# C and B loaded in pairs of chunks, first loads reordered, V loaded once, first products on VectorE

## Chip, cores and metric

The kernel runs on one core of a Trainium2 chip. The metric is the device time of one execution in microseconds. The times before are the median of three runs.

## What is computed

A Mamba-like mixer of 4 batches, 8 heads, 768 tokens, head width 32 and state width 16 works in chunks of 32 tokens; two feed-forward stages of width 1024 follow, the second after a mixing of the tokens through U and V of rank 32.

```python
# mixer, chunk by chunk: la = log(a)
L = np.exp(cum[:, :, :, None] - cum[:, :, None, :]) * causal
CB = np.einsum('bhin,bhjn->bhij', Cc, Bc)
y_intra = np.einsum('bhij,bhjd->bhid', CB * L, xc)
y_inter = np.einsum('bhin,bhnd->bhid', Cc, state) * decay_to_i[:, :, :, None]
state = decay_full[:, :, None, None] * state + np.sum(Bx, axis=2)
# first feed-forward stage
xn = (x - mu) / np.sqrt(var + 1e-06) * g_ln
x = x + np.maximum(xn @ w_ch1, 0.0) @ w_ch2
# second stage
h = x.transpose(0, 2, 1) @ U @ V
u = x + h.transpose(0, 2, 1)
out = u + np.maximum(u @ w_ch1, 0.0) @ w_ch2
```

The weights, U and V come as 64-bit floats, and the kernel turns them into 32-bit ones; the two stages' weights and V are then split into a high and a low part.

## The kernel before, in words

Everything is one list of work items. `Plan.add` (L81) takes a name, an engine, a planned cost, a function that issues the instructions, and the items it waits for. `Plan.issue` (L90) runs a small model of the engines, picks the item that is due first among those that could start soon, and calls its function: the order that it finds is the order of the instructions on every engine, and each engine works through its own in that order. A load is planned with a cost on SP's queue and one on a shared wire (`sp`, L49); constants such as `LAT`, `PER` and `SHIFT` (L41, L54) belong to this model alone. `FIRST` (L28) gives the first loads due times ahead of all others, in that order; those in `ACTQ` (L31) are issued from ScalarE's queue. `POOL` (L33) lists the items that GpSimd does instead of VectorE. Up to a planned time of 28 us the plan puts fillers (`dummy`, L997) on TensorE wherever its next item is planned more than 0.5 us ahead (L155 to L159); their number is fixed when the program is built.

The 768 tokens of a batch are 6 chunks of 128, so there are 24 chunks. In the first two batches (`FINE`) a chunk is worked in two halves of 64 tokens. For a chunk `bc` brings the decays into `lt` or, for the first two chunks, from `r` through a product into `bcp` (L557), after a clip and a memset on `r` (L405, L568); `scan` (L601) runs along them; `cb` (L610) multiplies C and B from `stk`; `mult` (L622) makes `mm` from both; `bw` (L634) and `stm` (L708) are the products for the state; `state` (L679, into `sps`) and `intra` (L657, L664, into `yps`) are the products on TensorE; `tps`, `mean`, `var` turn the result and take its moments.

`stk` before is two tiles, for even and odd chunks. Three loads fill one for a chunk (L577 to L584): B for 32 rows, and C for the even and the odd heads beside zeros that `stkz` has written once. The load of chunk k waits for `cb` of chunk k-2. For batches 2 and 3 the same tiles are cleared again (`stk0`) and filled from stacks in memory.

A weight piece is converted by `to_f32` (L295): the load into one of three `raw` slots, `a` on ScalarE, `s` (a shift, L315), `o` and `f` (L319) on VectorE. `w1_piece` of the first layer goes through TensorE (`pc`, L341 and L354) with `gd` and `gm`; the others are split on ScalarE and VectorE. V (L384 to L397) is loaded four times into the four groups of 32 rows, for each half. `ra` and `rcb` (L428 to L438) are the decays and C in rows of head and state; a clip (L405) and a scan (L447) on VectorE and a copy into `starts` on GpSimd (L442) belong to them.

The feed-forward stages run as `mm1` (L818, `hps`), `hh` and `hl` (L825, L829) and `mm2` (L843, L849, `acc`), interleaved over the batches by `ORDER` (L37).

## Time and profile before

| | us |
|---|---|
| median of three runs | 387.43 (387.12 to 388.31) |
| the profiled execution | 387.38 |
| its span | 385.5 |
| TensorE busy | 371.6 |
| VectorE busy | 249.7 |
| ScalarE busy | 154.2 |
| GpSimd busy | 10.1 |

The span runs from the first to the last instruction. PE is TensorE's matmuls, PEld its weight loads, DVE VectorE, ACT ScalarE, POOL GpSimd, SP the engine whose queue issues most loads. L and a number name a line of the kernel. PEclk is the granted clock of TensorE as a share of 2.4 GHz. A float32 product shows as two matmul instructions.

### The profile page before, as it was taken

What the parts mean: (1) busy time and instruction counts of PE and PEld (TensorE: products, weight loads), DVE (VectorE), ACT (ScalarE), POOL (GpSimd) and SP (SyncE); (2) the same over time, 40 slices, a digit from 0 to 9 for tenths busy, and PEclk for the clock granted to TensorE, in tenths of its full rate; (3) what the DMA queues carried; (4) which work ended last, traced back from release to release, by engine and by line L of the source; (5) the groups of instructions that cost most, each with busy time, mean ns of one, the idle gap of its engine ahead of it and who ended that gap; (6) DMA issues with size and microseconds to landing.
All of it is one profiled execution on the core that took longest, in us unless ns stands there. A gap on an engine that the chain in (4) does not pass through costs nothing.

```text
span 385.5 us, 8399 instructions
## 1 busy us (share of the span) xinstructions
PE 371.6 (96%) x3389; PEld 318.8 (83%) x3389; DVE 249.7 (65%) x512; ACT 154.2 (40%) x402; POOL 10.1 (3%) x28
## 2 busy tenths in 40 slices
PE   5999899989999999999999999999999999999996
PEld 2787788778888879998987779999878789998895
DVE  5798879989973894683563889258942742434232
ACT  3173653464634632433422541235432561233231
POOL 2202000000000100000000000000000000000000
PEclk9999999969999999999999999999999999999999
DMA  5776770656020683680032442219120010000010
GB/s 153 247 229 205 211 211 21 184 148 199 26 98 11 247 320 116 199 308 3 18 106 81 135 133 86 94 33 266 41 61 0 32 45 2 0 2 28 2 54 30
DMA packets 32243, 42.23 MB, mean 110 GB/s; under 512 B 4248, under 2 KB 21448, under 8 KB 32204
## 3 DMA queue, kind: packets, MB, share of 16 engines
q1 hardware_dynamic: 31772, 41.33, 34.6%
q8 instruction: 27, 0.44, 0.4%
q10 hardware_dynamic: 432, 0.37, 0.3%
q14 instruction: 12, 0.10, 0.1%
HBM read 33.72 MB, written 7.95 MB: 108 GB/s over the span
## 4 chain that ended last, share of the span: by engine, by line
PE 76%; DVE 12%; DMA 8%; issue 2%; ACT 1%; SPq 0%; ACTq 0%; DVEq 0%
PE hps L818 30%; PE acc L849 16%; PE acc L843 15%; DVE lt L601 3%; DMA lt<-arows 3%; DMA raw<-in_w 2%; PE yps L664 2%; DVE hl L829 2%; DMA rcb<-in_cbT 2%; PE cb L610 2%; DVE w L319 2%; PE cb L615 1%; PE ups L929 1%; DVE mm L622 1%; DMA ra<-in_a_rep 1%
## 5 line engine op out<-in xcount | busy, mean ns | idle before, releaser
L829 DVE SCALAR_TENSOR_TENSOR hl<-hps,hh 128x256 fp32r<-128x256 f32 (+1 forms) x128 | 70.4, 552 | 94.2 <-ACT hh L825 94.1
L825 ACT ACTIVATE hh<-hps 128x256 fp32r<-128x256 f32 (+1 forms) x128 | 62.6, 490 | 142.1 <-PE hps L818 127.1
L818 PE MATMUL hps<-yhl,w 128*128 128x512 f32 (+1 forms) x384 | 78.5, 341 | 0.3 <-DVE yhl L233 0.3
L818 PE MATMUL hps<-uhl,w 128*128 128x256 f32 (+1 forms) x384 | 77.1, 339 | 0.0
L843 PE MATMUL acc<-w,hh 128*128 128x256 f32 x384 | 73.6, 287 | 0.3 <-DVE w L233 0.3
L849 PE MATMUL acc<-hh,w 128*128 128x512 f32 (+1 forms) x256 | 73.5, 339 | 0.0
L818 PEld LDWEIGHTS hps<-uhl,w 128*128 128x128 f32 x384 | 61.0, 190 | 8.9 <-issue 1.0
L843 PEld LDWEIGHTS acc<-w,hh 128*128 128x128 f32 x384 | 62.2, 193 | 4.8 <-ACT hh L825 1.3
L818 PEld LDWEIGHTS hps<-yhl,w 128*128 128x128 f32 x384 | 59.5, 190 | 7.1 <-DVE yhl L233 0.7
L843 PE MATMUL acc<-w,hl 128*128 128x256 f32 x192 | 55.0, 286 | 1.0 <-DVE hl L829 1.0
L849 PEld LDWEIGHTS acc<-hh,w 128*128 128x128 f32 x256 | 46.2, 190 | 5.6 <-ACT hh L825 0.4
L601 DVE TENSOR_TENSOR_SCAN lt<-lt,eye 128x512 f32<-128x512 f32 x34 | 41.1, 1216 | 5.0 <-DMA lt<-arows 4.9
L849 PE MATMUL acc<-hl,w 128*128 128x512 f32 (+1 forms) x128 | 43.2, 337 | 0.1
L843 PEld LDWEIGHTS acc<-w,hl 128*128 128x128 f32 x192 | 37.0, 193 | 1.5 <-DVE hl L829 1.4
L849 PEld LDWEIGHTS acc<-hl,w 128*128 128x128 f32 x128 | 24.3, 190 | 2.5 <-DVE hl L829 0.3
L622 DVE TENSOR_TENSOR mm<-cb,lt 128x512 f32<-128x512 f32 x36 | 23.7, 684 | 1.6 <-PE cb L615 0.8
L319 DVE SCALAR_TENSOR_TENSOR w<-raw,w 128x512 int32<-128x512 int32 (+2 forms) x38 | 24.5, 650 | 0.1
L230 ACT ACTIVATE w<-raw 128x512 f32<-128x512 f32 (+2 forms) x19 | 12.2, 643 | 13.1 <-DMA raw<-in_w 8.6
L664 PE MATMUL yps<-mm,xt 128*32 128x64 f32 (+1 forms) x576 | 16.3, 246 | 1.2 <-issue 1.2
L610 PE MATMUL cb<-stk 32*64 32x128 f32 x192 | 14.4, 298 | 0.6 <-DMA stk<-in_cbT 0.6
L664 PEld LDWEIGHTS yps<-mm,xt 128*32 128x32 f32 x576 | 10.9, 112 | 4.0 <-issue 1.5
L610 PEld LDWEIGHTS cb<-stk 32*64 32x64 f32 x192 | 11.8, 147 | 2.6 <-issue 1.1
(101 smaller groups left out, 354.2 us busy)
## 6 DMA issues: line engine op xcount, KB each, us to landing
raw<-in_w SPq DMA_DIRECT2D x16, 512.0 KB, 4.6
lt<-arows SPq DMA_DIRECT2D x12, 512.0 KB, 4.7
stk<-st SPq DMA_DIRECT2D x48, 96.0 KB, 2.4
st<-sh SPq DMA_DIRECT2D x8, 384.0 KB, 8.1
xt<-in_xb SPq DMA_DIRECT2D x14, 192.0 KB, 3.3
lt<-arows SPq DMA_DIRECT2D x20, 128.0 KB, 4.3
out<-u SPq DMA_DIRECT2D x8, 256.0 KB, 2.1
xt<-in_xb SPq DMA_DIRECT2D x20, 96.0 KB, 3.2
```

The source lines that it names most:

```text
L230: A.activation(out=out, in_=in_, func=AF.Copy, **kw)
L319: V.scalar_tensor_tensor(out=t, in0=words(w), scalar=scalar, in1=t, op0=op, op1=ALU.bitwise_or)
L601: V.tensor_tensor_scan(t, pair[k] if k < 2 else t, eye, 0.0, op0=ALU.mult, op1=ALU.add)
L610: P.matmul(p[r_, 2 * q * w_:2 * (q + 1) * w_], t[:32, q, 0, r_], t[:32, q, 1:3, r_], start=True, stop=True, skip_group_check=True)
L615: P.matmul(p[:, 2 * q * C:2 * (q + 1) * C], stk[k % 2][:, pr, 0, :], stk[k % 2][:, pr, 1:3, :], start=True, stop=True)
L622: V.tensor_tensor(out=mm_[k][:, s_], in0=cbp[k, hf], in1=lt[k][:, s_], op=ALU.mult)
L664: P.matmul(p[32 * q:32 * q + 32, e, cols], x_[:, xh:xh + D], mm_[k][:, h * w_:(h + 1) * w_], start=q not in begun, stop=True, skip_group_c ...
L818: P.matmul(p[:, :n], w[:, k, fs], x[:, k, :], start=(i == 0), stop=(i == 5))
L825: A.activation(out=hh[:, :n], in_=hps[l, key, f][:, :n], func=AF.Relu)
L829: V.scalar_tensor_tensor(out=hl[:, :n], in0=hps[l, key, f][:, :n], scalar=0.0, in1=f32(hh[:, :n]), op0=ALU.max, op1=ALU.subtract)
L843: P.matmul(p, x[:, t * C:(t + 1) * C], w[:, f, :], start=(f == 0 and i == 0 and t % 2 == 0), stop=(f == NF - 1 and i == 2), skip_group_che ...
L849: P.matmul(accs[l, key][d][:, :n], w[:, f, ds_], x[:, :n], start=(f == 0 and i == 0), stop=(f == NF - 1 and i == 2))
```

## The change

- `stk` becomes one tile of four strips of 32 rows, each with the two chunks of a pair side by side. Three loads fill a strip for two chunks, and the odd chunk has no load of its own. `stkz` clears the tile's zeros, one half on VectorE and one on GpSimd. The load of a pair waits for `cb` of the chunks seven and eight back. `cb` reads its strip.
- `FIRST` is reordered and has two more loads; the first piece of `w1` is issued from ScalarE's queue, after `ra` and `rcb`.
- V is loaded once into 32 rows, converted there, and ScalarE writes its high part twice.
- `bw` and `stm` of chunks 0 and 1 move from GpSimd to VectorE; `starts` and a `stk` memset move to GpSimd, two memsets of `xt` to VectorE.
- The model's constants change, and it counts the loads in flight; the first items may be waited for longer.

Empty lines are left out of the diff.

```diff
--- before.py
+++ after.py
@@ -25,12 +25,12 @@
 FINE = sum(n == 2 for n in NS)
 PARTS = ((0, 2), (2, NC))
-FIRST = [('bc0', 0), 'cst0', ('stk', 0), ('ra', 0, 0), ('stk', 1), (('w1', 0, 0), 'ld'), ('xb', 0), ('rcb', 0, 0), 'cst',
-         'rows', (('w2', 0, 0), 'ld'), (('w1', 0, 1), 'ld')]
-ACTQ = ['cst0', ('ra', 0, 0), ('rcb', 0, 0)]
-POOL = {'rac': (), 'bw': (0, 1, 3, 4), 'stm': (0, 1, 4, 2)}
+FIRST = [('bc0', 0), 'cst0', ('ra', 0, 0), ('rcb', 0, 0), ('stk', 0), ('xb', 0), (('w1', 0, 0), 'ld'), 'cst', 'rows',
+         (('w2', 0, 0), 'ld'), (('w1', 0, 1), 'ld'), ('ra', 0, 2), ('stk', 2)]
+ACTQ = ['cst0', ('ra', 0, 0), ('rcb', 0, 0), (('w1', 0, 0), 'ld')]
+POOL = {'rac': (), 'bw': (3, 4), 'stm': (4, 2)}
 PE_SPLIT = ()
 YT = (2, 2)
@@ -38,7 +38,7 @@
          "000 001 010 101 011 020 100 111 021 110 030 121 031 120 131 130".split()]
-LAT, PER, T0, NEAR, SWITCH, STAY = 0.2308, 1.1979, 14.0, 0.2, 0.11, 3.0
+LAT, PER, T0, NEAR, SWITCH, STAY = 0.294, 1.1979, 14.0, 0.2, 0.047, 3.18
 dve = lambda n: 0.065 + n / 960
 scn = lambda n: 0.06 + n / 480
 dve2 = lambda n: 0.065 + n / 1920
@@ -46,12 +46,14 @@
 act = lambda n: 0.093 + n / 1200
 actp = lambda n: 0.051 + n / 1200
 pool_tt = lambda n: 0.0024 * n
-sp = lambda n, kb: (0.5 * n, kb / 360)
+sp = lambda n, kb: (0.5 * n, kb / RATE)
+RATE, FLIGHT = 290, 8
 SP_FIRST, SP_LAST = 0.65, 0.92
-SHIFT = dict(zip("rows w0 w1 w2 ra0 ra chunk0 chunk".split(), [-0.01, -2.48, 0.87, 6.97, -1.94, -0.4, -0.61, -1.17]))
+FIRST_NEAR = 2.0
+SHIFT = dict(zip("rows w0 w1 w2 ra0 ra chunk0 chunk".split(), [1.23, -2.48, 1.08, 6.97, -1.61, -2.81, -0.61, -1.17]))
 def kind(n):
@@ -114,7 +116,7 @@
         for i, n in enumerate(FIRST):
             items[n]["due"] = -1e3 + i
         lag = lambda it: (sum(it["cost"]) + SP_FIRST + SP_LAST if it["dma"] else it["cost"] + LAT)
-        wire = 0.0
+        wire, sent = 0.0, []
         for n in topo:
             it = items[n]
             if it["due"] is None:
@@ -146,7 +148,8 @@
                     continue
                 near = min(starts)[0] + NEAR
                 stay = lambda n: STAY if eng == "PE" and (n[0][:2] == "mm") == self.mode else 0.0
-                pick = min((items[n]["due"] - stay(n), i, t, n) for t, i, n in starts if t <= near)
+                pick = min((items[n]["due"] - stay(n), i, t, n) for t, i, n in starts
+                           if t <= near or items[n]["due"] < -900 and t <= near + FIRST_NEAR)
                 if best is None or pick[2] < best[0]:
                     best = (pick[2], eng, pick[3])
             assert best, [n for names in ready.values() for n in names][:20]
@@ -161,9 +164,13 @@
             if it["ring"]:
                 slots[it["ring"]].remove(min(slots[it["ring"]]))
             if it["dma"]:
-                free[eng] = t + it["cost"][0]
-                wire = max(wire, t + 0.5 + SP_FIRST) + it["cost"][1]
-                end = max(wire, free[eng] + SP_FIRST) + SP_LAST
+                m, now = round(it["cost"][0] / 0.5), t
+                for _ in range(m):
+                    now = max([now] + sent[-FLIGHT:][:1] * (len(sent) >= FLIGHT)) + 0.5
+                    wire = max(wire, now + SP_FIRST) + it["cost"][1] / m
+                    end = wire + SP_LAST
+                    sent.append(end)
+                free[eng] = now
             else:
                 cost = it["cost"]
                 if eng == "PE":
@@ -254,12 +261,21 @@
         return weights[l, i]
     stk = {}
-    def stk_zero(eng, i, rows, dt):
-        stk[i] = const.tile([96, 4, 3, C], dt, tag=f"stk{i}", name=f"stk{i}")
-        eng.memset(f32(stk[i])[:rows, :, 1:3, :], 0.0)
+    def stk_zero(eng, i):
+        if "n" not in stk:
+            stk["n"] = const.tile([96, 2, 4, 3, C], F32R, tag="stk", name="stk")
+            for j in range(2):
+                stk[j] = stk["n"][:, j]
+        eng.memset(f32(stk[i])[:, :, 1:3, :], 0.0)
+    def pairs_zero(eng, e):
+        if "f" not in stk:
+            stk["f"] = const.tile([128, 4, 3, 2 * C], F32, tag="stk", name="stp")
+        eng.memset(stk["f"][:, :, 1 + e, :], 0.0)
     def setup():
-        add("starts", "DVE", 0.5, lambda: V.memset(starts, 0.0))
+        add("starts", "Pool", 0.7, lambda: G.memset(starts, 0.0))
         add("zero", "DVE", 0.2, lambda: V.memset(zero, 0.0))
         add("cst0", "SP", sp(1, 104), lambda: load(out=cst[:, :202], in_=consts[:, :202]))
         add("cst", "SP", sp(1, 164), lambda: load(out=cst[:, 202:522], in_=consts[:, 202:522]), ["cst0"])
@@ -275,7 +291,7 @@
                 ["cst" if n == 1 else "cst0", "table"] + [("scan", k, 0) for k in range(first)])
         for i in range(3):
             for e in range(2):
-                add(("xz", i, e), "Pool", 0.3, lambda i=i, e=e: G.memset(
+                add(("xz", i, e), "DVE" if i == 1 else "Pool", 0.3, lambda i=i, e=e: (V if i == 1 else G).memset(
                     xt3[64 - 64 * e:128 - 64 * e, i, e * XW:e * XW + DM], 0.0))
         add("ng", "ACT", act(2), lambda: copy(ng, gsb, scale=-1.0 / DM), ["cst0", "table"])
@@ -288,11 +304,11 @@
                 [("gm", k), "cst"])
         add("negi", "ACT", act(C), lambda: copy(negi, ident, scale=-1.0), ["cst", "table"])
         for i in range(2):
-            add(("stkz", i), "DVE", 1.0, lambda i=i: stk_zero(V, i, 32, F32))
-            add(("stk0", i), "Pool", 1.0, lambda i=i: stk_zero(G, i, 96, F32R), [("cb", FINE * NC - 2 + i, 0)])
-    def to_f32(name, n, ld, kb):
+            add(("stkz", i), ("DVE", "Pool")[i], 1.0, lambda i=i: pairs_zero((V, G)[i], i))
+            add(("stk0", i), "Pool", 1.0, lambda i=i: stk_zero(G, i), [("cb", FINE * NC - 1 - j, 0) for j in range(2)])
+    def to_f32(name, n, ld, kb, rows=128):
@@ -304,10 +320,10 @@
             ld(cell["r"])
         def words(w):
-            return cell["r"][:, :2 * n].rearrange("p (n w) -> p n w", w=2)[:, :, w]
+            return cell["r"][:rows, :2 * n].rearrange("p (n w) -> p n w", w=2)[:, :, w]
         def scale():
-            cell["t"] = wst_p.tile([128, 512], F32, tag="w32", name="w32", bufs=2)[:, :n]
+            cell["t"] = wst_p.tile([128, 512], F32, tag="w32", name="w32", bufs=2)[:rows, :n]
             copy(cell["t"], words(1).bitcast(F32), scale=2.0 ** -112)
         def shift():
@@ -318,7 +334,7 @@
             t = cell["t"].bitcast(I32)
             V.scalar_tensor_tensor(out=t, in0=words(w), scalar=scalar, in1=t, op0=op, op1=ALU.bitwise_or)
-        add((name, "ld"), "SP", sp(4 if kb == 393 else 1, kb), alloc, ring="raw")
+        add((name, "ld"), "SP", sp(1, kb), alloc, ring="raw")
         add((name, "a"), "ACT", act(n), scale, [(name, "ld"), "table"], ring="w32")
         add((name, "s"), "DVE", dve2(n), shift, [(name, "a")])
         add((name, "o"), "DVE", dve(n), lambda: merge(1, -0x80000000, ALU.bitwise_and), [(name, "s")])
@@ -383,17 +399,19 @@
             frees=[("u", "a")])
         for hf in range(2):
             def ld(r, hf=hf):
-                for i in range(4):
-                    load(out=r[32 * i:32 * i + 32, :S], in_=v_w[:, hf * S:(hf + 1) * S])
+                load(out=r[:RK, :S], in_=v_w[:, hf * S:(hf + 1) * S])
             name = ("v", hf)
-            vc = to_f32(name, S // 2, ld, 393)
+            vc = to_f32(name, S // 2, ld, 98, RK)
             cs = slice(hf * S // 2, (hf + 1) * S // 2)
-            add((name, "h"), "ACT", act(S // 2), lambda vc=vc, cs=cs: copy(vs[:, cs], vc["t"]), [(name, "f")])
+            def hi(vc=vc, cs=cs):
+                for q in (0, 2):
+                    copy(vs[32 * q:32 * q + 32, cs], vc["t"][:RK])
+            add((name, "h"), "ACT", 2 * act(S // 2), hi, [(name, "f")])
             def lo(vc=vc, cs=cs):
                 for q in (1, 3):
-                    r_ = slice(32 * q, 32 * q + 32)
-                    sub(V, vs[r_, cs], vc["t"][r_, :], f32(vs[r_, cs]))
+                    sub(V, vs[32 * q:32 * q + 32, cs], vc["t"][:RK], f32(vs[:RK, cs]))
             add((name, "l"), "DVE", 2 * dve(S // 2), lo, [(name, "h")], frees=[(name, "a")])
@@ -574,14 +592,21 @@
             add(("bc", k), "SP", sp(ns, 524 / ns), bcast, ["a2d"] + gone)
         made = [("stk", k)]
         if b < FINE:
+            pr_, col = k // 2, k % 2 * C
+            strip = slice(32 * (pr_ % 4), 32 * (pr_ % 4) + 32)
             def ld_stk():
-                t = stk[k % 2]
-                view = cbT[b].rearrange("(q e n) w s -> e n q w s", e=2, n=N)[:, :, :, :, c * C:(c + 1) * C]
-                load(out=t[:32, :, 0, :], in_=cbT[b].rearrange("(q p) w s -> p q w s", p=32)[:, :, 1, c * C:(c + 1) * C])
+                t = stk["f"][strip]
+                cols = slice(c * C, (c + 2) * C)
+                view = cbT[b].rearrange("(q e n) w s -> e n q w s", e=2, n=N)
+                load(out=t[:, :, 0, :], in_=cbT[b].rearrange("(q p) w s -> p q w s", p=32)[:, :, 1, cols])
                 for e in range(2):
-                    load(out=t[16 * e:16 * e + 16, :, 1 + e, :], in_=view[e][:, :, 0, :])
-            add(("stk", k), "SP", sp(3, 131), ld_stk, [("stkz", k % 2)] + prev("cb", 2, 0))
+                    load(out=t[16 * e:16 * e + 16, :, 1 + e, :], in_=view[e][:, :, 0, cols])
+            if k % 2 == 0:
+                add(("stk", k), "SP", sp(3, 262), ld_stk, [("stkz", e) for e in range(2)] + prev("cb", 8, 0) + prev("cb", 7, 0))
+            else:
+                alias["stk", k] = ("stk", k - 1)
         else:
             def ld_stk():
                 view = stacks[b].rearrange("w (e p n) g s -> e (n g) p w s", e=2, p=4)
@@ -603,11 +628,12 @@
         def cb(hf):
             p = cbp[k, hf] = ps_m.tile([128, 512], F32, tag="m", name="cb")
             if b < FINE:
-                t = stk[k % 2]
+                t = stk["f"][strip]
                 for q in range(4):
                     for i in range(ns):
                         r_ = slice(i * w_, (i + 1) * w_)
-                        P.matmul(p[r_, 2 * q * w_:2 * (q + 1) * w_], t[:32, q, 0, r_], t[:32, q, 1:3, r_],
+                        cols = slice(col + i * w_, col + (i + 1) * w_)
+                        P.matmul(p[r_, 2 * q * w_:2 * (q + 1) * w_], t[:, q, 0, cols], t[:, q, 1:3, cols],
                                  start=True, stop=True, skip_group_check=True)
                 return
             for q in range(4 // parts):
```

## Rows read from the trace of the kernel before

**Rows 1.** The page: busy time, share of the span and instructions of each engine.

```profile
PE 371.6 (96%) x3389; PEld 318.8 (83%) x3389; DVE 249.7 (65%) x512; ACT 154.2 (40%) x402; POOL 10.1 (3%) x28
```

**Rows 2.** The windows: length, each engine's busy us, granted clock, DMA share, GB/s.

```profile
0.00:20.00 20.00, 16.14 (x104) 10.28 (x105) 13.02 (x27) 4.44 (x9) 4.66 (x18) 1.00 0.68 203
...
20.00:75.00 55.00, 52.93 (x771) 45.61 (x771) 49.03 (x102) 29.26 (x75) 3.59 (x8) 1.00 0.60 173
...
75.00:85.00 10.00, 7.29 (x159) 6.01 (x154) 8.42 (x24) 5.47 (x17) 0.00 (x0) 0.66 0.64 174
...
140.00:225.00 85.00, 85.00 (x637) 74.30 (x636) 52.05 (x102) 32.42 (x87) 0.00 (x0) 1.00 0.43 139
```

**Rows 3.** The chain of waits, 0 to 20 us: start, length, what.

```profile
1.15 4.62 DMA ra<-in_a_rep
...
6.17 3.78 PE bcp L557 x4
...
9.95 0.75 PE dummy L997 x3
...
10.70 3.61 PE cb L610 x32
...
14.30 1.18 PE dummy L997 x5
...
16.50 2.28 PE dummy L997 x11
...
18.78 1.30 PE pc L341 x6
```

**Rows 4.** The timeline of TensorE, 30 to 40 us: start, length, work, [idle before].

```profile
30.78 1.09 PE L610 MATMUL cb<-stk 32*64 32x128 f32 x16 [0.60 <-DMA stk<-in_cbT]
...
39.96 0.65 PE L664 MATMUL yps<-mm,xt 128*32 128x64 f32 x30 [1.17 <-issue]
```

**Rows 5.** The chain of waits at 72 us.

```profile
72.37 3.96 DMA raw<-in_w
```

**Rows 6.** The timeline of VectorE and TensorE at 77 us.

```profile
77.11 0.43 DVE L315 TENSOR_SCALAR w<-w 128x512 int32<-128x512 int32 x1 [0.58 <-ACT w L230]
...
78.19 0.65 PE L679 MATMUL sps<-xt,bw 128*32 128x64 f32 x16 [2.03 <-DVE mm L622]
```

**Rows 7.** The windows of 1 us: 82 to 83 us.

```profile
82.00:83.00 1.00, 1.00 (x7) 1.00 (x7) 0.96 (x5) 0.67 (x3) 0.00 (x0) 0.50 0.50 115
```

**Rows 8.** The DMA issues: count, KB each, median us from issue to landing.

```profile
stk<-in_cbT SPq DMA_DIRECT2D x12, 64.0 KB, 5.1
...
cst<-in_consts ACTq DMA_DIRECT2D x1, 101.0 KB, 2.2
```

**Rows 9.** The timeline of SP's queue and TensorE, 2 to 7 us.

```profile
2.06 5.09 SPq L215 DMA_DIRECT2D stk<-in_cbT  x6
...
3.20 2.31 PE L997 MATMUL dummy<-zero 128*128 128x256 bf16 x10 [3.20 <-DVE zero L263]
```

**Rows 10.** Groups of instructions: busy us, mean ns of one, idle before.

```profile
L634 DVE TENSOR_TENSOR bw<-xt,lt 128x128 f32<-128x128 f32 x8 | 2.3, 286 | 0.5 <-DMA xt<-in_xb 0.5
...
L708 DVE TENSOR_TENSOR stm<-gst,cst 128x128 f32<-128x128 f32 x6 | 1.7, 286 | 0.1
...
L259 DVE MEMSET stk<- 32x1024 f32 x2 | 1.8, 912 | 1.2 <-PEq L1040 1.0 <-issue 0.2
...
L262 DVE MEMSET starts<- 128x768 f32 x1 | 0.7, 698 | 0.1
...
L278 POOL MEMSET xt<- 64x256 f32 x6 | 1.8, 306 | 0.5 <-POOLq L1040 0.3
...
L230 ACT ACTIVATE vs<-w 128x384 fp32r<-128x384 f32 x2 | 1.1, 526 | 3.8 <-DVE w L319 3.8
```

**Rows 11.** The timeline of SP's queue, 12 to 46 us.

```profile
12.64 1.28 SPq L215 DMA_DIRECT2D stk<-in_cbT  x3
...
44.13 1.92 SPq L215 DMA_DIRECT2D raw<-in_v_w  x4
```

## The prediction

> **What bounds the kernel now.** I read the busy shares first: TensorE is busy 96% of the span [rows 1], so the time is its work plus what it loses. The table by stretches says where it loses [rows 2]: from 140 to 225 us it is busy 85.00 of 85.00, while it is idle 3.9 us of the first 20, 2.07 of the next 55 and 2.71 between 75 and 85. Only these stretches have something to give, and VectorE is the second busy engine there (49.03 of 55 from 20 to 75).
>
> The chain of waits then says what the first 20 us are [rows 3]. The load of `ra` is issued at 1.15 and lands 4.62 later, at 5.77; its clip sits in VectorE's order ahead of the memset on `r` that the first product `bcp` needs, so `bcp` starts at 6.17. From there to `pc` at 18.78 TensorE works without a gap, but 19 of its instructions are fillers (`dummy`), 0.75 + 1.18 + 2.28 = 4.21 us of the chain. Fillers are issued by count, so they hold up what stands behind them even if it is ready. TensorE is slow here, whatever the clock column prints for this stretch: 32 `cb` products take 3.61 us, while later 16 take 1.09 [rows 4], and a filler of the last eleven takes 2.28 / 11 = 0.207.
>
> In the middle I read two gaps [rows 4]: 0.60 us for a load of `stk`, 1.17 us ending at 39.96. The granted clock of that stretch is 1.00 [rows 2]. The costly place is at 76 us. A weight load of the second layer is issued at 72.37 and takes 3.96 [rows 5]. VectorE stands 0.58 us at that piece's shift (L315), which begins at 77.11; the product `mm` that frees the bank for TensorE's `sps` is queued behind it, and `sps` waits 2.03 us [rows 6]. The clock falls to 0.50, the level of 1.2 GHz [rows 7]. Its mean over 75 to 85 us is 0.66 [rows 2], so 10 x 0.34 / 0.5 = 6.8 us are spent at that level; some 2.4 of them are idle, and the work in the other 4.4 loses half, 2.2. With the 2.71 us idle the place costs 4.9.
>
> **The change part by part.** The profiled execution took 387.38 us, its span of 385.5 and 1.9 around it; the median of the runs shown is 387.43. The sum is made from 387.4.
>
> *First loads.* `ra` and `rcb` now go ahead of the 512 KB piece of `w1` on ScalarE's queue instead of beside it. `ra` can hardly land sooner than the constants ahead of it do, 2.2 after issue [rows 8], so 3.35, and no later than now, 5.77. I take about 4, nearer to the constants' row, since only 128 KB more stand ahead of its end. The Trainium skill, page "DMA: Bandwidth & Descriptors", section "Queues, rings and completion order", says that each DMA engine takes one queue's descriptors in ring order and alternates between queues. By it `ra` comes some 1.5 us sooner; if only the sum of bytes counted it would come at 5.77 and this term would be nothing; no row here shows `ra` without the weight beside it.
>
> `bcp` also stands behind the first fillers: ten from 3.20 on, 2.31 us [rows 9]. By the planner's constants the load of `r` ends at 0.5 + 0.65 + 8/290 + 0.92 = 2.10, its clip 0.60 and a wait of 0.29 later; then the clip of `ra` 0.20 and the memset 0.07 + 0.29 bring `bcp` to 3.56, and (3.56 - 0.5 - 1.0) / 0.213 makes ten fillers again. So `bcp` starts at 3.20 + 2.31 = 5.5: 0.7 us gained; between 0 (the load as late as now) and 0.9 (the memset ahead of the clip, nine fillers).
>
> *Products to VectorE.* `bw` and `stm` take 0.286 us each there [rows 10]. Four products add 1.14; two memsets on `xt` add 2 x 0.27 (0.912 for 1024 elements against 0.698 for 768 makes 0.84 ns for an element and 0.06 besides; GpSimd takes 0.306 for one). One memset on `stk` (0.91) and the one on `starts` (0.70) leave: about +0.1 in all. VectorE is idle 7 of the first 20 us [rows 2], which covers it; without that cover it costs the 1.14, since the memsets that leave lie ahead of anything late. GpSimd's memsets (0.91, four of 0.31, 0.70) follow each other from 0.74 to about 3.8 and are over when `ra` lands. What moves with the products is the number of fillers: the plan counts 0.198 for a product on VectorE and 0.307 on GpSimd, two in a row, so 0.22 us or two fillers of 0.107 fewer, 0.4 us as they run. Its bounds are wide: all 19 gone, -4.2; and with `w1` fourth in ScalarE's queue the plan expects it 1.0 + (524/290 - 524/360) = 1.35 us later, up to thirteen fillers more, +2.7. I take -0.4, since `pc` also waits for `gd`, which doesn't move.
>
> *Pairs of `stk`, V once.* The products stay as many and as large. On SP's queue three issues for a pair replace six, and each V half takes one issue instead of four. Six issues of `stk` took 5.09 us at the start [rows 9], three took 1.28 later, four of V 1.92 [rows 11]. Up to 56 us that is 12 issues of 0.43 to 0.85 and 6 of 0.48 fewer: 8 to 13 us of the queue's time. `xt`, `lt`, `rcb` and the weights stand behind them there and go sooner, and a pair's load waits for chunks seven and eight back instead of two. Against it: the first `cb` now needs the whole pair's load, behind memsets on two engines that end near 2.0; three issues of up to 0.85 and 5.1 to landing [rows 8] end between 7.1 and 9.7, and `cb` starts near 10, so this is just covered; at the late end and with `bcp` done at 9.3 it would cost 0.4. The gap of 0.60 goes, since its load is issued a chunk earlier. Of the other 1.47 us of gaps I take a fifth. Together -0.9, between +0.4 and -2.07. The V halves' second copy on ScalarE adds 2 x 0.526 [rows 10], beside an engine busy 29.26 of 55; at worst the next raw slot comes 1.05 us later.
>
> *The place at 76 us.* The plan now counts 0.5 + 0.65 + 524/290 + 0.92 = 3.88 us for a weight load, where it counted 3.53 and the trace shows 3.96. That should put `mm` ahead of the shift: it would run from 77.11 - 0.58 = 76.5 instead of 77.5, and the wait of 2.03 would be 1.1. After a gap of that size, 1.17 at 39.96, the clock did not fall. So 0.9 + 2.2 = 3.1 us, between 0 (the order stays) and 4.9.
>
> *A new order everywhere.* The dues and the model's constants change, so every engine's order may change after the first microseconds, and `stk`'s second tile is cleared for both chunks at once. The nearest row for what a fresh order leaves is the 2.07 us of gaps from 20 to 75; I charge half, 1.0, between 0 and the 4.9 of the place at 76.
>
> Sum: -0.7 - 0.4 - 0.9 - 3.1 + 1.0 = -4.1, so 383.3 us. Its own range, 381.5 to 386, goes from no charge for the order to the clock still falling.
>
> **The rivals.** *All of it closes:* no gap of note before 110 us: -0.9 - 0.4 - 2.07 - 4.9, so 379.1. For it speaks that SP's queue, which feeds all of these, loses 8 us or more of its first 56; against it, that VectorE stays busy 89% from 20 to 75.
>
> *It does not do what it says:* `ra` lands as late as now, or what is gained at the start comes back as gaps because VectorE, whose work is the same, is late next; the place at 76 stays, since V and U keep their raw slots until their conversions as now. Only the gap of 0.60 goes and the new order costs its 1.0: 387.4 - 0.6 + 1.0 = 387.8.
>
> *Slower, by the clock:* a second wait made by the order. The place is VectorE's queue between 20 and 110 us, where each conversion of a weight stands ahead of products for TensorE. If one more wait for a weight load keeps TensorE idle for 2 us, the clock goes to 0.50 as at 77 us, and that costs 4.9. With the place at 76 kept: 387.4 - 0.7 - 0.4 - 0.9 + 4.9 = 390.3. It decides from a gap between 1.17 us (no fall) and 2.03 us (fall). For it: products that GpSimd made on its own now stand in that queue; against: they are four, and early.
>
> **How the numbers follow.** Forecast 0.46, all closes 0.17, no effect 0.17, second fall 0.20. The range from 379.5 to 389.0 leaves out half of the first rival and somewhat more than half of the last, 0.2 together. A measurement of this kernel can tell about 0.3%, 1.2 us, from no change. Faster than 386.3 are the forecast but for 0.02, the first rival, and 0.05 of the second: 0.66. Within the bound are 0.14, slower 0.20.
>
> **What would show it.** `bcp` near 5.5 with ten fillers ahead of it, and `ra` landing near 4; 17 fillers from there to the first `pc`, which begins near 17.7 instead of 18.8; no wait of TensorE for `stk`; 18 issues fewer on SP's queue before 56 us; between 70 and 90 us no gap above 1.2 us and no clock of 0.50; from 140 us on as full as now. I would be wrong through a gap of 2 us with a fallen clock anywhere before 110 us, or through many more fillers ahead of `pc`.

## The result, and the profile after

The changed kernel takes 378.0 us, the median of four runs (376.44 to 378.8), against 387.27 for the kernel before, timed beside it. The ratio is 0.9751 with a 95% interval of 0.971 to 0.9792, so it is faster by 9.3 us. The forecast was 383.3 with a range from 379.5 to 389.0: the direction held, the size did not, and the time lies below the range. The profiled execution took 377.27 us with a span of 375.5, 10.0 less than the span before. The granted clock, averaged over the span, is 0.998 to 1.000 in the four executions, and 0.989 in the profiled one of the kernel before. Ratios leave out executions more than 1.5% above the fastest of their kernel, so a ratio is not always the quotient of two medians.

The page of the changed kernel: the busy time of each engine, and the shares of the chain of work that ended last, by engine; after it the first line of that chain's shares for the kernel before.

```profile
PE 368.0 (98%) x3398; PEld 317.5 (85%) x3398; DVE 248.0 (66%) x516; ACT 155.8 (41%) x404; POOL 10.6 (3%) x24
...
PE 94%; DVE 4%; issue 1%; ACT 0%; ACTq 0%
```

```profile
PE 76%; DVE 12%; DMA 8%; issue 2%; ACT 1%; SPq 0%; ACTq 0%; DVEq 0%
```

TensorE lost 385.5 - 371.6 = 13.9 us before [rows 1] and loses 7.5 now. The loads, 8% of the chain before, are no longer in it. The table by stretches of the changed kernel says where (columns as in [rows 2]):

```profile
0.00:20.00 20.00, 16.99 (x114) 11.08 (x114) 11.63 (x28) 4.89 (x10) 3.93 (x14) 1.00 0.93 235
20.00:75.00 55.00, 54.64 (x798) 46.61 (x796) 50.58 (x106) 32.06 (x83) 4.80 (x8) 1.00 0.60 173
75.00:85.00 10.00, 9.35 (x172) 8.21 (x173) 9.86 (x27) 6.11 (x18) 0.00 (x0) 1.00 0.47 142
...
225.00:230.00 5.00, 5.00 (x35) 4.62 (x34) 4.90 (x16) 1.20 (x2) 0.00 (x0) 1.00 0.05 17
...
270.00:280.00 10.00, 10.00 (x61) 8.07 (x60) 4.31 (x8) 4.43 (x12) 0.00 (x0) 1.00 0.22 61
```

Against [rows 2], the idle time of TensorE went from 3.86 to 3.01 us in the first 20, from 2.07 to 0.36 in the next 55, and from 2.71 to 0.65 between 75 and 85; there the granted clock is 1.00 where it was 0.66. Later too there is something that the prediction did not look for. The same view of the kernel before has three short gaps after 85 us, 0.34 + 0.66 + 0.39 = 1.39, which are gone (the lines are of the kernel before):

```profile
135.00:140.00 5.00, 4.66 (x23) 3.20 (x23) 5.00 (x9) 1.90 (x7) 0.00 (x0) 1.00 0.85 290
...
225.00:230.00 5.00, 4.34 (x25) 3.32 (x24) 5.00 (x13) 1.84 (x5) 0.00 (x0) 1.00 0.20 75
...
270.00:280.00 10.00, 9.61 (x73) 8.12 (x72) 9.78 (x17) 4.39 (x12) 0.00 (x0) 1.00 0.14 45
```

The start, in the timeline of TensorE of the changed kernel (start, length, work):

```profile
2.88 2.53 PE L1023 MATMUL dummy<-zero 128*128 128x256 bf16 x11 [2.88 <-DVE zero L279]
5.34 3.78 PE L575 MATMUL bcp<-r,cst 2*128 2x512 f32 x4
9.05 3.68 PE L636 MATMUL cb<-stp 32*64 32x128 f32 x32
12.66 3.60 PE L1023 MATMUL dummy<-zero 128*128 128x256 bf16 x18
...
17.54 0.70 PE L357 MATMUL pc<-w,gd 128*128 128x256 f32 x2
...
25.35 0.97 PE L844 MATMUL hps<-yhl,w 128*128 128x256 f32 x6
```

And the last of these in the kernel before:

```profile
25.28 0.96 PE L818 MATMUL hps<-yhl,w 128*128 128x256 f32 x6
```

`bcp` begins at 5.34 and `pc` at 17.54, close to the 5.5 and 17.7 that were forecast. But the first product of the feed-forward stage, `hps`, begins at 25.35, and it began at 25.28 before. The two timelines have the same products up to there, but for two of `tps` (four before, two now). What the start gained is gone by then: more fillers, 18 in a row before the first `sps` and 6 behind the first products of `pc`. So the whole gain of 10.0 us lies behind 25 us: idle time 1.71 + 2.06 + 1.39 + 0.38 (the last one at the end of the span) = 5.5, the work done at 1.2 GHz around 80 us 2.2, and 2.3 by which TensorE's busy time for the same work is shorter. No row tells where these 2.3 come from.

SP's queue of the changed kernel (start, time that the queue took to issue, what, count):

```profile
29.83 2.81 SPq L222 DMA_DIRECT2D stp<-in_cbT  x6
32.88 4.48 SPq L222 DMA_DIRECT2D lt<-arows  x4
...
44.58 2.25 SPq L222 DMA_DIRECT2D stp<-in_cbT  x3
...
52.29 0.83 SPq L222 DMA_DIRECT2D raw<-in_v_w  x2
```

All 18 issues of the pairs are out by 47 us, in 9.36 us of the queue's time (1.58, 1.37 and 1.35 at the start, and the rows shown), and the four loads of `lt` behind the fourth and fifth pair are asked for from 32.88 on.

### The profile page after: what moved, and what is told of

It reads as the page before. It is cut to its first block, busy times and chain, and to the rows that moved or that the text cites. A ratio compares the mean times of both kernels' runs of the same rounds, so it can differ in the third digit from the quotient of the medians.

```text
span 375.5 us, 8369 instructions
## 1 busy us (share of the span) xinstructions
PE 368.0 (98%) x3398; PEld 317.5 (85%) x3398; DVE 248.0 (66%) x516; ACT 155.8 (41%) x404; POOL 10.6 (3%) x24
## 2 busy tenths in 40 slices
DMA packets 30130, 41.63 MB, mean 111 GB/s; under 512 B 3864, under 2 KB 19528, under 8 KB 30092
## 4 chain that ended last, share of the span: by engine, by line
PE 94%; DVE 4%; issue 1%; ACT 0%; ACTq 0%
PE hps L844 35%; PE acc L875 18%; PE acc L869 17%; PE yps L690 4%; PE cb L636 3%; PE pc L357 2%; PE dummy L1023 2%; PE yps L683 2%; PE tps L772 2%; PE cb L641 2%; PE ups L955 2%; PE yps L676 1%; PE gps L916 1%; DVE hl L855 1%; PE bcp L575 1%
## 5 line engine op out<-in xcount | busy, mean ns | idle before, releaser
L869 PE MATMUL acc<-w,hh 128*128 128x256 f32 x384 | 72.6, 285 | 0.0
L869 PEld LDWEIGHTS acc<-w,hh 128*128 128x128 f32 x384 | 61.4, 191 | 3.3 <-DVE w L240 0.4
L237 ACT ACTIVATE yhl<-yps 128x256 fp32r<-128x256 f32 x24 | 9.2, 382 | 15.7 <-PE yps L690 15.6
L636 PE MATMUL cb<-stp 32*64 32x128 f32 x192 | 14.6, 298 | 0.0
L636 PEld LDWEIGHTS cb<-stp 32*64 32x64 f32 x192 | 11.8, 146 | 3.3 <-issue 2.7
```

Of the source, the lines that this page charges most:

```text
L237: A.activation(out=out, in_=in_, func=AF.Copy, **kw)
L636: P.matmul(p[r_, 2 * q * w_:2 * (q + 1) * w_], t[:, q, 0, cols], t[:, q, 1:3, cols], start=True, stop=True, skip_group_check=True)
L869: P.matmul(p, x[:, t * C:(t + 1) * C], w[:, f, :], start=(f == 0 and i == 0 and t % 2 == 0), stop=(f == NF - 1 and i == 2), skip_group_che ...
```

## The experiments

Two theories stood at first. *Order*: the gain comes from the planner's new model, which counts loads better and so finds a better order. *Parts*: it comes from what is physically removed, SP's issues above all. Ratios are to the kernel before on the same chip, which took 387.9 to 389.1 there.

### The model alone, the parts alone, the order alone

The kernel before with the changed kernel's model and nothing else:

```diff
-LAT, PER, T0, NEAR, SWITCH, STAY = 0.2308, 1.1979, 14.0, 0.2, 0.11, 3.0
+LAT, PER, T0, NEAR, SWITCH, STAY = 0.294, 1.1979, 14.0, 0.2, 0.047, 3.18
-sp = lambda n, kb: (0.5 * n, kb / 360)
+sp = lambda n, kb: (0.5 * n, kb / RATE)
+RATE, FLIGHT = 290, 8
+FIRST_NEAR = 2.0
...
+                for _ in range(m):
+                    now = max([now] + sent[-FLIGHT:][:1] * (len(sent) >= FLIGHT)) + 0.5
...
```

(`SHIFT` and the longer wait for the first items go with it, as in the change.)

> The kernel before with the planner's new model alone: its constants, dues, the count of loads in flight and the longer wait for first items; loads, tiles and engines as before. Order theory (the gain is the order of VectorE's and SP's queues that the new model finds): 379 to 382, no fall of the clock at 76 us. Parts theory (the gain is fewer issues and bytes, and the earlier start): 386 to 389, gaps as before.

It took 386.72 us, a ratio of 0.9948 (0.9915 to 0.9981). The timeline of TensorE shows a wait of the same size again, only later, and the window of 75 to 85 a granted clock of 0.89. What TensorE waits for is now `stm`, for VectorE makes the first `mm` of this place well ahead (second line):

```profile
81.72 0.42 PE L664 MATMUL yps<-ra,stm 32*32 32x64 f32 x16 [2.16 <-DVE stm L715]
...
65.22 0.68 DVE L629 TENSOR_TENSOR mm<-cb,lt 128x512 f32<-128x512 f32 x1
```

The opposite: the changed kernel with its loads, pairs, V and products, planned by the old constants.

```diff
-LAT, PER, T0, NEAR, SWITCH, STAY = 0.294, 1.1979, 14.0, 0.2, 0.047, 3.18
+LAT, PER, T0, NEAR, SWITCH, STAY = 0.2308, 1.1979, 14.0, 0.2, 0.11, 3.0
-sp = lambda n, kb: (0.5 * n, kb / RATE)
-RATE, FLIGHT = 290, 8
+sp = lambda n, kb: (0.5 * n, kb / 360)
-FIRST_NEAR = 2.0
...
```

> The changed kernel with the old model: pairs, V once, first loads and products as changed, but the old constants, dues and picking. Order theory: 385 to 388, with a wait of 2 us and a fallen clock left somewhere. Parts theory: 379 to 381.

It took 387.95, a ratio of 0.9982 (0.995 to 1.0013): nothing. TensorE waits again in several places, the longest at 81 us:

```profile
30.60 0.43 PE L698 MATMUL sps<-xt,bw 128*32 128x64 f32 x16 [1.33 <-issue]
...
80.91 0.43 PE L676 MATMUL yps<-ra,stm 32*32 32x64 f32 x16 [1.97 <-DVE stm L727]
```

Third, the changed kernel's list and order, with the parts undone inside it: each pair loaded by six issues, V by four, the products of chunks 0 and 1 on GpSimd, the first piece of `w1` from SP.

```diff
-                load(out=t[:, :, 0, :], in_=cbT[b].rearrange("(q p) w s -> p q w s", p=32)[:, :, 1, cols])
-                for e in range(2):
-                    load(out=t[16 * e:16 * e + 16, :, 1 + e, :], in_=view[e][:, :, 0, cols])
+                for j in range(2):
+                    cols, at = slice((c + j) * C, (c + j + 1) * C), slice(j * C, (j + 1) * C)
+                    load(out=t[:, :, 0, at], in_=cbT[b].rearrange("(q p) w s -> p q w s", p=32)[:, :, 1, cols])
+                    for e in range(2):
+                        load(out=t[16 * e:16 * e + 16, :, 1 + e, at], in_=view[e][:, :, 0, cols])
...
```

(The other three are the diffs of the single runs below.)

> The changed kernel in its own order of items, planned as it is, but what the items issue is as before: six issues for a pair of stk, four for a V half with one copy on ScalarE, the first four products on GpSimd, the first w1 piece from SP's queue. Order theory: 378 to 380. Parts theory: 383 to 387, with waits of TensorE for loads between 20 and 80 us and bcp at about 6.2.

It took 384.38, a ratio of 0.9903 (0.9876 to 0.993). So neither half does it: the model alone is worth 0.5%, the parts under the old model 0.2%, the new order without the parts 1.0%, and all together 2.5%. The two theories were put as rivals, and both fall in that form: the order pays in full only if the queue can keep it. What stops it is in the trace of this third run, 12 issues of the strips in 9.32 us on SP's queue from 32.08 on with `lt` behind them, and a wait of 4.94 us of TensorE at 47.67. The next runs take the parts one by one.

### Which part carries it

Only the pair's load by six issues instead of three, all else as changed (the diff above and nothing else):

> The changed kernel in its own order; only the load of a pair is issued as six transfers, three for each chunk, in place of three: 18 issues more on SP's queue, same bytes. Queue theory (what the undone kernel lost, some 6 us, is SP's queue with the row of twelve stk issues ahead of the decay loads lt): 382 to 384, VectorE waiting 3 us or more for lt near 42 us and the clock falling. If the bytes of V or the products on GpSimd were the loss: 377 to 378.5.

It took 385.39, a ratio of 0.9944 (0.9916 to 0.9971); this one part, undone, takes back 0.9944 - 0.9751 = 1.9%, some 7 us of the 9.3; against the three single runs below, which were timed on the same chip, it is 1.4 to 1.5%. SP's queue, VectorE and TensorE of this run:

```profile
32.13 1.12 SPq L222 DMA_DIRECT2D raw<-in_w  x2
33.31 8.29 SPq L222 DMA_DIRECT2D stp<-in_cbT  x12
41.70 3.06 SPq L222 DMA_DIRECT2D lt<-arows  x4
```

The twelve issues from 33 to 42 us, each one's time in ns (least, median, most), and what the queue itself waited for there (us in total, times, longest):

```profile
L222 SPq DMA_DIRECT2D stp<-in_cbT x12: 311/428/494, 33.3 to 41.2; - x12
...
SPq L222 <- DMA raw<-in_w: 2.9, 2, 2.1
```

```profile
46.02 1.23 DVE L627 TENSOR_TENSOR_SCAN lt<-lt,eye 128x512 f32<-128x512 f32 x1 [4.19 <-DMA lt<-arows]
...
48.72 0.29 DVE L661 TENSOR_TENSOR bw<-xt,lt 128x128 f32<-128x128 f32 x1 [1.15 <-DMA xt<-in_xb]
```

```profile
49.11 0.44 PE L706 MATMUL sps<-xt,bw 128*32 128x64 f32 x8 [5.06 <-DVE bw L661]
```

```profile
20.00:75.00 55.00, 48.52 (x707) 41.16 (x705) 44.17 (x92) 27.85 (x75) 3.77 (x8) 0.94 0.58 169
```

Here the mechanism can be read from end to end. Twelve issues hold the queue for 8.29 us. The issues themselves are 12 x 0.43, some 5 us of it; for 2.9 us the queue stands still, because its seventh and eighth issue (at 36.98 and 39.41) wait for the landing of the two weight loads that were issued eight places ahead of them, at 32.13 and 32.76. The planner's model has this too: `FLIGHT` counts eight loads. In the changed kernel the row at this place has six issues, 2.81 us, and the queue waits 0.2. So the first load of `lt` behind them is issued at 41.70 instead of 32.88. VectorE's scan waits 4.19 us for these loads, then `bw` 1.15 for an `xt` that stands still further back; TensorE's `sps` waits 5.06 for `bw`. Behind that wait the granted clock falls: 0.94 over 55 us is 55 x 0.06 / 0.5 = 6.6 us at 1.2 GHz. TensorE is idle 6.5 us there, against 0.36 in the changed kernel. The bytes are the same in both; the number of issues differs, 36 against 18, and with it the size of the pieces (31954 packets in all against 30130), which no run varies alone.

V alone by four issues into 128 rows, as before:

```diff
-                load(out=r[:RK, :S], in_=v_w[:, hf * S:(hf + 1) * S])
+                for i in range(4):
+                    load(out=r[32 * i:32 * i + 32, :S], in_=v_w[:, hf * S:(hf + 1) * S])
```

> The changed kernel in its own order; only V is loaded as before, four issues for a half into 128 rows and one copy on ScalarE. Queue theory: 377.5 to 378.5, since these issues stand late, at 52 us, where the queue runs ahead. If V's issues and bytes carry the gain: 381 or more, with gaps of TensorE between 50 and 80 us.

378.66, a ratio of 0.9798 (0.9745 to 0.9851).

The products of chunks 0 and 1 alone on GpSimd:

```diff
-        add(name, "Pool" if pooled else "DVE", pool_tt(n) if pooled else cost, lambda: fn(G if pooled else V), *args, **kw)
+        add(name, "Pool" if pooled else "DVE", pool_tt(n) if pooled else cost,
+            lambda: fn(G if pooled or what != "rac" and which in (0, 1) else V), *args, **kw)
```

> The changed kernel in its own order; only bw and stm of chunks 0 and 1 run on GpSimd. Each takes 0.2 to 0.4 us longer. If the start is not on the path, as ten more fillers without a loss say: 377.5 to 378.5. If the products' place matters: 379 to 380.

377.92, a ratio of 0.9792 (0.973 to 0.9854).

The first piece of `w1` alone from SP's queue:

```diff
-            queue.append(A)
+            queue.append(A if len(seen) < 3 else nc.sync)
```

> The changed kernel in its own order; only the first piece of w1 is issued from SP's queue, behind the pair of stk, in place of ScalarE's. Queue theory: 378 to 379, one issue of 0.4 us more on SP's queue. If w1's arrival beside ra matters: 380 or more, bcp at 6.

379.45, a ratio of 0.9807 (0.9758 to 0.9855). Each of these last three is within 0.6% of the changed kernel's 0.9751, and each interval overlaps with that of the changed kernel (0.971 to 0.9792): they may cost some tenths of a per cent, and no more can be said. Six more issues for V cost far less than 18 more for the pairs, and no `lt` stands close behind them at 52 us.

### The queue in the old order

If SP's queue is the cause, the pairs should pay in the kernel before too, without any new plan. Its own order was kept: the load of the odd chunk keeps its place in the list and issues nothing, and the even one brings both.

```diff
+            def ld_stk():
+                if k % 2:
+                    return
+                t = stk["f"][strip]
+                cols = slice(c * C, (c + 2) * C)
...
             add(("stk", k), "SP", sp(3, 131), ld_stk, [("stkz", k % 2)] + prev("cb", 2, 0))
```

> The kernel before in its own order of items; only stk is one tile of strips, loaded for two chunks by three issues where the even chunk's load stood, and the odd chunk's load is nothing. If SP's queue alone was the loss: 381 to 384. If fewer issues help only in an order that uses them: 386 to 388, with the wait and the fallen clock at 76 us as before.

It took 383.89, a ratio of 0.988 (0.9827 to 0.9932): half of the whole gain, with no new order, no new constant and the old first loads. The profiled execution is the shortest of the five, 382.16 us. Its windows, VectorE and TensorE:

```profile
20.00:75.00 55.00, 54.20 (x785) 46.85 (x783) 51.84 (x107) 31.45 (x79) 3.59 (x8) 1.00 0.62 180
75.00:85.00 10.00, 9.53 (x186) 8.24 (x182) 9.83 (x28) 6.30 (x20) 0.00 (x0) 1.00 0.68 203
```

```profile
73.98 0.43 DVE L324 TENSOR_SCALAR w<-w 128x512 int32<-128x512 int32 x1 [0.55 <-ACT w L230]
74.33 0.68 DVE L637 TENSOR_TENSOR mm<-cb,lt 128x512 f32<-128x512 f32 x1
```

```profile
76.41 0.43 PE L672 MATMUL yps<-ra,stm 32*32 32x64 f32 x16 [0.47 <-DVE stm L723]
```

The costly place is closed in this execution. The shift still stands ahead of `mm` and still waits 0.55 us, but it comes at 73.98 instead of 77.11 [rows 6]: the weight that it converts has its turn 3 us sooner. TensorE waits 0.47 instead of 2.03, and the granted clock stays at 1.00. From where the 3 us come can be read 20 us earlier, first in the kernel before, then in this run:

```profile
46.62 2.05 SPq L215 DMA_DIRECT2D stk<-in_cbT  x3
...
51.99 0.37 SPq L215 DMA_DIRECT2D ra<-in_a_rep  x1
...
56.65 0.56 DVE L405 TENSOR_SCALAR ra<-ra 128x768 f32<-128x768 f32 x1 [2.44 <-DMA ra<-in_a_rep]
```

```profile
50.25 0.38 SPq L215 DMA_DIRECT2D ra<-in_a_rep  x1
...
53.55 0.56 DVE L414 TENSOR_SCALAR ra<-ra 128x768 f32<-128x768 f32 x1
```

Before, three issues of `stk` stand ahead of a load of `ra`, and VectorE waits 2.44 us for that load. Without them it is issued at 50.25 instead of 51.99 and lands in 3.3 us at most instead of 4.66, VectorE does not wait, and from there to the shift all its work comes 3.1 us sooner (53.55 for 56.65, 73.98 for 77.11), while TensorE's `cb` in front of the place comes only 0.6 sooner (72.37 for 72.95). Of the five executions two have a mean granted clock of 1.000, 382.16 and 382.32 us; the others, 383.89 to 387.09, have 0.991 to 0.994, so some of their work ran at 1.2 GHz, and where is not on record.

The same with the new model and the pairs planned as such, but first loads, products, `starts` and V as before:

```diff
-FIRST = [('bc0', 0), 'cst0', ('stk', 0), ('ra', 0, 0), ('stk', 1), (('w1', 0, 0), 'ld'), ('xb', 0), ('rcb', 0, 0), 'cst',
+FIRST = [('bc0', 0), 'cst0', ('stk', 0), ('ra', 0, 0), (('w1', 0, 0), 'ld'), ('xb', 0), ('rcb', 0, 0), 'cst',
...
+            if k % 2 == 0:
+                add(("stk", k), "SP", sp(3, 262), ld_stk, [("stkz", e) for e in range(2)] + prev("cb", 8, 0) + prev("cb", 7, 0))
+            else:
+                alias["stk", k] = ("stk", k - 1)
...
```

> The kernel before with the new model and with pairs of stk, planned as such; first loads (but for the odd chunk's), products on GpSimd, starts and V as before. If pairs and the new model together are the gain: 377 to 381. If the order of the first loads, V once or the products are needed: 383 to 386.

It took 383.85, a ratio of 0.9888 (0.9844 to 0.9932), no better than the pairs in the old order. Other waits have come (waits of TensorE: engine, line, what it waited for, us in total, times, longest), and the clock falls again: its mean is 0.97 from 20 to 75 us and 0.99 from 140 to 280.

```profile
PE tps L773 <- ACT yc L237: 2.4, 1, 2.4
...
PE sps L706 <- DVE bw L661: 1.9, 1, 1.9
```

So some 1.4% of the change needs the rest of it, first loads and small parts, under the new model. Undone singly inside the finished order, these cost little; taken out before the planning they cost that much. Which of them it is was not tried, and that it is one of them is not shown either: the plan finds another order for any list, and no run shows how far the time moves by that alone, for instance with the model's constants changed a little. The same holds for the 0.5% and the 0.2% of the first two runs.

### What the start is worth

Ten more fillers ahead of `bcp`, to see whether its start is on the path:

```diff
+            for _ in range(10 if k == 0 else 0):
+                plan.filler()
```

> The changed kernel with ten more fillers ahead of bcp, 2.1 us of TensorE's time. If the start is on the path to the end (TensorE bound from there on): 380.0, 2 us slower. If VectorE or the loads set the pace of the first 100 us: 378 to 378.7, and the 1.1 us that bcp and pc come earlier were worth nothing either.

It took 377.71, a ratio of 0.9755 (0.9711 to 0.98), the same as the changed kernel. The run does not answer the question as it was put, for the fillers did more than delay. Timeline of TensorE, then windows:

```profile
2.88 3.82 PE L1025 MATMUL dummy<-zero 128*128 128x256 bf16 x21 [2.88 <-DVE zero L279]
6.63 1.98 PE L577 MATMUL bcp<-r,cst 2*128 2x512 f32 x4
```

```profile
6.00:13.00 7.00, 7.00 (x50) 4.79 (x48) 4.87 (x10) 1.67 (x3) 0.13 (x2) 0.72 0.93 248
13.00:20.00 7.00, 6.83 (x63) 4.61 (x61) 3.69 (x11) 0.88 (x2) 0.00 (x0) 0.79 1.08 261
```

`bcp` starts 1.3 us later but takes 1.98 instead of 3.78, and ends sooner. So the start was pulled the other way, by leaving out the 21 fillers that stand between `cb` and the second product of the state (fillers compute nothing that is used):

```diff
+    def filler():
+        done.append(1)
+        if not 11 < len(done) <= 32:
+            P.matmul(dummy, zeros[:, :C], zeros, start=True, stop=True)
```

> The changed kernel without the 21 fillers between cb of the first two chunks and pc. VectorE waits 3.85 us for sps, which stands behind 18 of them. If that chain sets the time: 375 to 376, pc some 3 us sooner. If the fillers raise the clock, and without them the first 20 us run longer at the low level, or if VectorE's later work holds TensorE anyway: 377.5 to 380.

It took 380.41, a ratio of 0.979 (0.9749 to 0.9831), no faster and perhaps slower. The profiled execution is the shortest of six, 377.23 us. Its timeline of TensorE, the window of 20 to 75 us, and two waits of VectorE from 20 to 77 us (us in total, times, longest):

```profile
14.23 1.22 PE L357 MATMUL pc<-w,gd 128*128 128x256 f32 x2 [0.50 <-DVE gd L302]
...
22.84 0.98 PE L844 MATMUL hps<-yhl,w 128*128 128x256 f32 x6
...
42.18 0.32 PE L705 MATMUL sps<-xt,bw 128*32 128x64 f32 x8 [1.56 <-issue]
```

```profile
20.00:75.00 55.00, 52.42 (x715) 45.10 (x708) 47.78 (x100) 29.72 (x78) 2.74 (x6) 1.00 0.66 173
```

```profile
DVE lt L626 <- DMA lt<-arows: 2.4, 2, 1.4
DVE bw L660 <- DMA xt<-in_xb: 1.7, 1, 1.7
```

The first `hps` comes 2.5 us sooner, and between 20 and 75 us TensorE is idle 2.58 instead of 0.36: the 2.5 us are given back nearly whole (2.2), and the span is 375.4 against 375.5. VectorE waits 2.4 us for `lt` and 1.7 for `xt`, waits that the changed kernel does not have there: in this stretch the loads set the pace, and an earlier start only waits for them. The other five executions took 379.74 to 381.34 us, with a mean granted clock of 0.989 to 0.995 where this one has 0.999, so in these some work ran at 1.2 GHz besides.

Both edits together:

> As the run before, with ten fillers more ahead of bcp, which in an earlier run let bcp take 1.98 us in place of 3.78. If the clock's early rise lasts: 374 to 376. If it falls again while TensorE waits: 377.5 to 381.

378.73, a ratio of 0.9739 (0.9699 to 0.978), like the changed kernel; it waits 2.03 us at 39.70. No version beat the changed kernel by more than the intervals hold.

## Why the prediction was right or wrong

*What bounds the kernel.* Right that TensorE's idle time is what can be won, and that the place at 76 us is the largest piece. Wrong that only the first 85 us have something to give: 1.39 us of short gaps lay behind, beside the one full stretch, 140 to 225 [rows 2], from which the prediction judged all that follows.

*First loads.* The sizes held, the worth did not. `ra` landed 3.4 us after its issue at 1.16, so at 4.56 (about 4 was taken, between 3.35 and 5.77), `bcp` began at 5.34 (5.5), behind eleven fillers (ten). By the Trainium skill, page "DMA: Bandwidth & Descriptors", section "Queues, rings and completion order", `ra` ahead of the weight on one ring was to come about 1.5 us sooner, as the prediction estimated; it came 1.21 sooner, but no run here shows that the ring's order did it. The weight was also issued 0.97 later, at 2.12 instead of 1.15, and where it went out on SP's queue at 2.79 or 4.20 (the `w1` run and the run with all parts undone), `ra` landed at 4.08 and 3.68, sooner still. But 0.8 us at 5 us is worth nothing at 25, as the equal starts of `hps` show, and the run without 21 fillers shows that even 2.5 us there are not kept. The failed step is that a gain at the start was put on the path that sets the end, though the loads of the next 50 us do not move with it.

*Products to VectorE.* Seventeen fillers between `bcp` and `pc` were forecast, 21 came. `pc` at 17.54 is near the 17.7, and its worth is again nothing. The products alone, put back on GpSimd, change no more than the interval of that run.

*Pairs of `stk`, V once.* This is the step that failed most. The price was taken from the gaps of TensorE that SP's queue showed between 20 and 75 us, a fifth of 1.47 and the 0.60, at 0.9 in all. The queue's own time came out in its range, in part by luck: 8 to 13 us fewer were forecast up to 56 us, and 15.87 + 3.84 - 9.36 - 0.83 = 9.5 came (the time of all issues of `stk` and V on it up to 56 us, before and after), from 12 issues fewer rather than 18, since all pairs now come that early. The price of 0.85 for an issue was misread: in the 5.09 us of [rows 9] the queue waits 2.0 us for `ra` and 0.7 for `rcb` to land, and the six issues take 0.31 to 0.43 each. What was wrong above all is its worth. In the old order the pairs alone are worth 1.2%, 4.7 us, most of it, in the profiled execution 2.2 + 2.2 of 5.1, at a place that the prediction put down to something else; in the new order 18 more issues cost 1.4 to 1.9%. A queue in order delays everything behind it, and the delay shows up later as a wait for another engine: some 8 us later by way of `stp`, `lt`, scan, `bw` and `sps` in that run, over 20 us later by way of `stk`, `ra` and the shift in the kernel before. The row of a gap names the last link alone. V's part could not be told from nothing.

*The place at 76 us.* The size was nearly right: 3.1 was taken with a bound of 4.9, and 2.06 + 2.2 = 4.3 came. The reason was wrong, so the size is luck. The planner's better estimate of a weight load was to put `mm` ahead of the shift. `mm` did move ahead, to 59.12 in the changed kernel and 65.22 with the new model alone, but to 61.12 with the old constants too, and it was not what TensorE waited for in the end: with the model alone it still waits 2.16 us, at 81.72, now for `stm`, and the clock falls. VectorE is late as a whole there; it waits 3.1 us for `ra` in that run, 2.44 in the kernel before. In the old order, the shift still ahead, fewer issues on SP's queue take that wait away and close the place. Nor do the pairs close it in every order: planned with the old constants it is back, 1.97 us at 80.91.

*A new order everywhere.* Charged 1.0 us; the sign was wrong in this case. The new order and the parts together are better than the sum of each alone (0.5% and 0.2%), and it closed the gaps behind 85 us: in every kernel with the changed order, the undone ones too, TensorE is busy 140.00 of the 140 us from 140 to 280, with the other orders 137.26 to 139.01. But that a new order can cost as much as was charged, the run with the new model and planned pairs shows: two new waits of 2.4 and 1.9 us and two falls of the clock.

*The rivals.* "All of it closes", 379.1 with 0.17, was nearest: its argument, that SP's queue feeds all of these places, is what the runs bear out. Measured by it, the start gave 1.3 us less, gaps of 0.36 and 0.65 stayed, and 1.39 behind 85 us, 0.38 at the end and the unexplained 2.3 of busy time came on top. It was held down because VectorE is busy 89% between 20 and 75 us; it is busier now, 50.58 of 55, and TensorE does not wait for it there. "Slower by the clock" did not happen, but its mechanism did in several experiments: behind waits of 1.97, 2.16, 4.94 and 5.06 us the clock fell, and behind 0.96 at 75.65 in the changed kernel and 1.56 at 42.18 in the run without 21 fillers it did not.

*What stays open.* The 2.3 us of busy time; the 1.3% between the pairs alone and the whole change, and whether it hangs on first loads, V or products, or on the order that the plan happens to find.

## What to carry to other kernels

Price an issue on a queue in order by what stands behind it, not by the gaps that name it, and look at what the queue itself waits for before its row is divided by its issues: list the loads behind it with the work that waits for each, and ask what all of them arriving some microseconds sooner would close, also later and on other engines. Before a gain at the start is counted, look for what paces the middle; where loads do, an earlier start comes back as gaps. When a change has a planner's model and physical parts in it, each alone can be worth nothing and both together most, so neither test alone decides.

## What the runs showed of the hardware

- Twelve issues of `stp` in a row held SP's queue for 8.29 us: 0.43 us for an issue (0.31 to 0.49), and 2.9 us in which the queue waited for two loads issued eight places ahead to land. The Trainium skill, page "DMA: Bandwidth & Descriptors", section "Issuing engines are not separate DMA queues", calls the time on the sequencer to start a transfer "usually small relative to the DMA itself". For one transfer the trace agrees, 0.43 us against 5.1 from issue to landing. But the load that stands behind such a row waits for all of it, and with 18 more issues the kernel took 385.39 instead of 378.0.
- 21 fillers in a row instead of 11 were followed by a `bcp` in 1.98 us instead of 3.78, so TensorE reached the level of 2.4 GHz already there; then it fell back, the granted clock being 0.72 from 6 to 13 us and 0.79 from 13 to 20. Over the whole kernel it gained nothing. The column shows 1.00 for the first microseconds of every run, where `bcp` of four products takes 3.78 us as well as 1.98, so it is no measure of the level there.
